# An attention block gated by a gated feed-forward block on one core: x blocks, first weights and value runs placed anew

## The chip, the cores and the metric

The kernel runs on one core of one Trainium2 chip. The metric is the device time of one execution in microseconds (us). A core has TensorE (PE, matrix products, results in PSUM), VectorE (DVE), ScalarE (ACT), GpSimd (POOL) and SyncE (SP, here only the issuer of DMAs). Each engine works through its own list in order; semaphores order the engines among each other.

## The reference

Two branches share one input x of 2048 rows by 576 columns, in bfloat16. The second input B_x is not read.

```python
xn = _layernorm(x)                                  # over the 576 columns
# branch A: causal attention, 32 heads of 18, window of 256
qkv = xn @ wqkv                                     # 576 x 1728
scores = einsum(q, k) * 18 ** -0.5                  # masked: 0 <= i - j < 256
s = (softmax(scores) @ v) @ wo                      # 576 x 576
# branch B: gated feed-forward, F = 4608
h = sigmoid(xn @ w_gate) * (xn @ w_up)
g = silu(h @ w_down)
out = x + s * g
```

## The kernel before

The 2048 rows are cut into four chunks of 512 rows, each of four blocks of 128. For each chunk the program makes: the layer norm and the transposed copy `xnT` of its blocks; q, k and v; scores, exponentials and masks per group of four heads; the products of probabilities and values, called runs here (`build_pv`, L817); the output projection; the gate and up products over 36 blocks of 128 feed-forward columns (`build_ffn`); the down products; and the final combination and store.

All contractions over the 576 columns are split into one remainder of 64 and four groups of 128. A matmul uses half of the array's rows (64), and two of them run side by side as a pair (`pair`, L127), so one line of the kernel, L127, carries nearly all products. `turn` does the four main groups first (half 0) and, in a second call (half 1), the four groups again with the halves swapped, and the remainder last. The remainder's columns of x lie twice in `xnT`, once for each half of the array: that is what `ln:dup` (L561) makes by copying 64 columns of the normalized block (`xnr`).

**The order of the work** is not written by hand. Every operation is an `Op` with an engine, an estimated time, dependencies, a priority and, for PE, a PSUM buffer that it must get from a `Pool`. `schedule` plays the program through with these estimates and fixes each engine's list. A lower `prio` goes first among operations that could start at about the same time. SP's list of DMAs comes from the same planner, with an estimated issue time and an estimated landing (`slack` corrects it). There are four PSUM units: 0 and 1 for scores and the like, 2, 3 and 1 for the feed-forward part.

**The opening.** In the first chunk x comes by four DMAs (`load_x`, x0 to x3). Each block goes through statistics (L541 to L547 on DVE; x2's on ACT, `act_stats`, L600 to L604), the inverse root on POOL (L549), the normalization (L557), the copy of 64 columns (L561), ten transposes on PE (L613: five groups times two halves) and one copy from PSUM to `xnT` (`f_xe`, L590; ACT for x0 to x2, DVE for x3). Until then PE multiplies zeros (`warm`). The first two feed-forward blocks (`NEARLY`) are made one x block at a time (`PARTS`), each part as soon as its x block is there; the third block follows over all 512 rows, with its half 0 started ahead. Gate and up weights come in groups of two feed-forward blocks (`weights`, two loads of 256 KB), their remainders for four blocks (`load_rem`, two loads of 64 KB). SP's order at the start is x0, x1, x2, x3, gate and up of group 0, two remainders, gate and up of group 1, two remainders of the next four blocks, group 2, group 3, then the attention weights.

**The runs.** Two runs per chunk, eight in all, each of 192 matmuls and as many weight loads (128 in the first chunk's). They are short instructions, so a run uses up instructions faster than any other work. Instructions come in blocks of 256 through a DMA queue of their own (66 blocks of 16 KB in the trace). `fits` refuses a start of a run if, by the planner's estimate, too little time lies between a fixed point 256 + 64 instructions ahead of a block's edge and the edge itself (`FETCH_NS`, the second value near the end of a chunk's gate and up products).

Of the kernel before, what the change touches and what calls it, by code (L numbers as in the profile page):

```python
# [7 lines left out]
S = 2048  # L8
# [37 lines left out]
FETCH_NS = (6200.0, 4350.0)  # L46
RUN_NS = 6.3
STEP_NS = (54.0, 30.6)
# [21 lines left out]
X_PRIO = (0, 0, 0, 0)  # L70
# [22 lines left out]
FILL_NS = 100.0  # L93
SPACE_NS = (1700, 1800, 1700, 1700)
# [62 lines left out]
class Pool:  # L157
# [12 lines left out]
    def pick(self, n, now, barred=()):  # L170
        free = []
        for u in self.units:
            if u in barred:
                continue
            h = self.last[u]
            if h is None:
                free.append((0.0, self.units.index(u), u))
            elif h.rel and all(r.idx >= 0 for r in h.rel):
                free.append((max(now, max(r.end for r in h.rel) + self.late), self.units.index(u), u))
        if len(free) < n:  # L180
            return None
        free.sort()
        got = free[:n]
        return max(g[0] for g in got), sorted(g[2] for g in got)
# [11 lines left out]
class Op:  # L196
    __slots__ = ("eng", "est", "deps", "fn", "name", "prio", "start", "end", "tok", "needs_tok",
                 "nbytes", "slack", "idx", "succs", "cidx", "odeps", "acq", "lane", "filler", "space", "ni", "run", "then")

    def __init__(self, eng, est, fn, name, deps, prio, nbytes, odeps, acq):  # L200
# [33 lines left out]
        self.then = None  # L234
        for d in self.odeps:
            assert d.eng == eng
# [22 lines left out]
class Builder:  # L259
# [40 lines left out]
    def alloc_memory(self):  # L300
# [61 lines left out]
        self.pool_f = Pool("F", [2, 3, 1], last)  # L362
        self.pool_v = Pool("V", [0, 1, 2, 3], last)

    def build_graph(self):
# [16 lines left out]
        self.op_xnT = [[] for _ in range(NC)]  # L382
        self.op_v = {}
# [60 lines left out]
    def load_rem(self, dst, srcs, name, lane, prio, deps=()):  # L444
        return [self.dma(dst[ROWS[1 - t], :], src[0:RD, :], RD * src.shape[1] * 3, name, lane + (t,), deps=deps, prio=prio)
                for t, src in enumerate(srcs)]

    def build_consts(self):
# [15 lines left out]
        self.warm(NWARM[0], z, None, 107)  # L464
# [60 lines left out]
    def build_ln(self, c):  # L525
# [3 lines left out]
        for i in range(BPC):  # L529
# [41 lines left out]
            self.ln_dup = dup  # L571
            self.r_st.release(ss, ap)
# [6 lines left out]
            h = self.pool_s.hold()  # L579

            def f_tr(eng, h=h, sn=sn):
                return self.transposes(eng, h, lambda r, o: self.xnr[r, sn, o:o + P])
            tr = op("PE", KB * 29.5, f_tr, f"tr:{st}", deps=[ap, dup, self.op_ident, war], prio=0, acq=h, ni=20)
            self.r_xn.release(sn, tr)
            if i == 0:
                self.warm(NWARM[1], None, tr, 80)

            def f_xe(e, h=h, i=i):
                dst = self.xnT[:, xs, :, i * P:(i + 1) * P].rearrange("p k (t c) -> p t k c", t=2)
                return e.activation(dst, self.tr_src(h), ACTF.Copy) if e is self.nc.scalar else e.tensor_copy(dst, self.tr_src(h))  # L590
            eng = XE_ENG[i]
            xe = op(eng, dve_ns(KB * P, 1.9) if eng == "DVE" else act_ns(KB * P), f_xe, f"xe:{st}", deps=[tr], prio=0)
            h.release(xe)
            self.op_xnT[c].append(xe)

    def act_stats(self, x_in, o_x, pr):
# [4 lines left out]
        m = op("POOL", 150, lambda e: e.tensor_scalar(nm, sx, -1.0 / D, None, ALU.mult), "ln:am", deps=[a1], prio=pr)  # L601
# [740 lines left out]
```

## Time and profile before

| | |
|---|---|
| time, median of 3 runs | 556.4 us (556.1 to 556.68) |
| profiled execution | 556.48 us, span 555.2 us |
| PE busy | 549.9 us, 99% |
| DVE, ACT, POOL busy | 325.1, 271.7, 208.8 us |
| data moved | 75.87 MB, mean 137 GB/s; 230 to 263 GB/s in the first 97 us |
| first gate and up product | 7.98 us after the span's start |
| last matmul ends | 552.7 us |

The span runs from the first to the last instruction; 1.3 us of the profiled execution lie around it. Durations of matmuls contain a modelled end, so matmuls overlap in the rows, and "busy" says that work was in flight, not that the array was full. A row of a timeline gives start, duration, engine, line, operation, output and input, shapes, the count of merged instructions, and in brackets the idle time before it and what ended it.

### The profile page before, as it was taken

To read this page: it belongs to the slowest core of one execution; us is meant where nothing else is said; L and a number is where in the kernel's file an instruction comes from. 1 tells how busy PE (TensorE), PEld (TensorE's weight loads), DVE (VectorE), ACT (ScalarE), POOL (GpSimd) and SP (SyncE) were. 2 spreads that over 40 slices of the span, in tenths; PEclk is the share of its full clock that TensorE was granted. 3 is DMA by queue.
4 is the path that set the end of the run, shared out by engine and by line. 5 is a ranking of instruction groups with operands and counts; after the bars stand their busy time and mean duration, and the time that the engine had idled before them with its cause. 6 is when DMAs were issued, how large, how long until landed. Compare 5 with 4: busy or idle time off the path is not lost.

```text
span 555.2 us, 19412 instructions
## 1 busy us (share of the span) xinstructions
PE 549.9 (99%) x8342; PEld 341.2 (61%) x8342; DVE 325.1 (59%) x782; ACT 271.7 (49%) x379; POOL 208.8 (38%) x360
## 2 busy tenths in 40 slices
PE   8999999999999999999999999999999999999998
PEld 7454455777555655577855565447877655445887
DVE  5467677745966545746565557664455657653511
ACT  4246554432566543645265563764165555765021
POOL 5634353826271230554452322745063332700300
DMA  8899999542256664462126653663013464540001
GB/s 230 234 263 239 248 241 257 150 91 59 72 164 182 198 167 132 129 161 53 32 65 193 201 162 101 185 179 87 9 34 103 119 204 138 153 134 2 20 28 46
DMA packets 141213, 75.87 MB, mean 137 GB/s; under 512 B 43676, under 2 KB 139260, under 8 KB 141128
## 3 DMA queue, kind: packets, MB, share of 16 engines
q1 hardware_dynamic: 133704, 68.71, 47.3%
q0 software_dynamic: 7424, 5.92, 4.0%
q8 instruction: 66, 1.08, 0.8%
q14 instruction: 19, 0.16, 0.1%
HBM read 63.18 MB, written 2.36 MB: 118 GB/s over the span
## 4 chain that ended last, share of the span: by engine, by line
PE 98%; DMA 1%; SPq 0%; issue 0%; DVE 0%; ACT 0%
PE ps L127 95%; PE ps L817 3%; DMA wgs<-in_B_w_up_dram 1%; SPq L290 0%; ACT thf L1087 0%; PE ps L613 0%; DVE thf L1089 0%; DVE xf L1092 0%
## 5 line engine op out<-in xcount | busy, mean ns | idle before, releaser
L127 PE MATMUL ps<-xnT,wgs 64*128 64x512 bf16 (+1 forms) x2400 | 284.0, 368 | 0.6 <-DMA wgs<-in_B_w_up_dram 0.5
L767 ACT ACTIVATE expr<-ps 128x1024 bf16<-128x1024 f32 (+4 forms) x160 | 155.0, 968 | 81.0 <-PE ps L127 80.5
L127 PEld LDWEIGHTS ps<-xnT,wgs 64*128 64x128 bf16 x2400 | 114.7, 94 | 108.6 <-issue 1.1
L127 PE MATMUL ps<-wd_sb,hT 64*128 64x288 bf16 (+2 forms) x2448 | 152.7, 276 | 0.0
L290 POOL DMA_DIRECT2D qk<-qd x160 | 82.9, 524 | 161.7 <-PE ps L127 152.9
L977 DVE SCALAR_TENSOR_TENSOR hT<-tring,ps 128x512 bf16<-128x512 bf16 x144 | 98.6, 685 | 74.2 <-ACT tring L974 72.6
L974 ACT ACTIVATE tring<-ps 128x512 bf16<-128x512 f32 x144 | 86.2, 598 | 113.9 <-PE ps L127 112.3
L127 PEld LDWEIGHTS ps<-wd_sb,hT 64*128 64x128 bf16 x2448 | 113.0, 94 | 29.4
L780 DVE TENSOR_TENSOR expr<-expr,mask 128x128 bf16<-128x128 bf16 (+2 forms) x240 | 65.2, 299 | 62.0 <-ACT expr L767 59.4
L290 POOL DMA_DIRECT2D oT<-o2T x72 | 36.8, 520 | 115.3 <-DVE ot L848 52.4
L731 POOL TENSOR_SCALAR kx<-kprev,small 128x256 bf16<-128x256 bf16 x64 | 60.1, 949 | 6.0 <-PE ps L127 5.1
L127 PE MATMUL ps<-qk,kx 64*128 64x320 bf16 (+1 forms) x704 | 59.2, 254 | 0.0
L127 PE MATMUL ps<-xnT,wgr 64*128 64x512 bf16 (+1 forms) x300 | 56.0, 367 | 0.0
L127 PEld LDWEIGHTS ps<-qk,kx 64*128 64x128 bf16 x704 | 31.9, 94 | 26.6
L127 PE MATMUL ps<-xnT,wqg 64*128 64x512 bf16 (+1 forms) x320 | 37.7, 355 | 0.0
L652 DVE CAST qd<-ps 128x1024 bf16<-128x1024 f32 (+1 forms) x20 | 22.3, 1115 | 11.1 <-PE ps L127 11.1
L845 DVE STREAM_TRANSPOSE ot<-ps 128x512 f32<-128x512 f32 x32 | 20.3, 687 | 13.9 <-PE ps L817 13.8
L127 PEld LDWEIGHTS ps<-xnT,wgr 64*128 64x128 bf16 x300 | 15.0, 94 | 16.4
L731 DVE TENSOR_SCALAR kx<-qk,small 128x512 bf16<-128x512 bf16 x64 | 21.9, 370 | 5.4 <-PE ps L127 4.9
L853 DVE STREAM_TRANSPOSE o2T<-o 128x512 bf16<-128x512 bf16 x32 | 22.6, 706 | 3.0 <-DMA oT<-o2T 2.5
L127 PEld LDWEIGHTS ps<-xnT,wqg 64*128 64x128 bf16 x320 | 15.0, 94 | 11.5 <-issue 0.4
L1080 ACT ACTIVATE thf<-ps 128x576 bf16<-128x576 f32 x12 | 7.8, 650 | 27.4 <-PE ps L127 27.4
(68 smaller groups left out, 289.3 us busy)
## 6 DMA issues: line engine op xcount, KB each, us to landing
wgs<-in_B_w_gate_dram SPq DMA_DIRECT2D x72, 256.0 KB, 3.5
wgs<-in_B_w_up_dram SPq DMA_DIRECT2D x72, 256.0 KB, 4.0
wd_sb<-in_B_w_down_dram SPq DMA_DIRECT2D x9, 576.0 KB, 6.7
wqg<-in_A_wqkv_dram SPq DMA_DIRECT2D x32, 128.0 KB, 3.8
qk<-qd POOLq DMA_DIRECT2D x100, 36.0 KB, 2.7
wgr<-in_B_w_gate_dram SPq DMA_DIRECT2D x36, 64.0 KB, 3.1
wgr<-in_B_w_up_dram SPq DMA_DIRECT2D x36, 64.0 KB, 2.9
wvo<-in_A_wqkv_dram SPq DMA_DIRECT2D x4, 576.0 KB, 4.2
```

Source lines behind the costliest of these rows:

```text
L127: res = eng.matmul(outs[i], lhs(ROWS[t], i), rhs(ROWS[t], i), start=start, stop=stop, tile_position=(64 * t, 0))
L290: o = self.op(eng, DMA_ISSUE_NS[eng], lambda e: e.dma_start(dst, src), name, deps, prio, nbytes=nbytes)
L652: return eng.tensor_copy(dst, self.both(h, n))
L731: return e.tensor_scalar(self.kx[:, sx, pos:pos + n_ // SW, t, :], src.rearrange("p (s k) -> p s k", k=SW), self.half[:, t:t + 1], None, A ...
L767: return eng.activation(self.expr[:, se, :, lo * SW:NT], self.both(h, NT)[:, :, lo * SW:NT], ACTF.Exp, scale=SM_SCALE)
L780: return eng.tensor_tensor(e_, e_, m_, ALU.mult)
L817: res = eng.matmul(outs[i][p0:p0 + VH, cols], self.v_aug[ROWS[i], o:o + VH], self.expr[ROWS[i], se, t, cols], start=m == 0, stop=m == len( ...
L845: return e.transpose(self.ot1[:, p1, :], self.halves(hp, NT, un)[i])
L853: t2 = op("DVE", dve_ns(NT), lambda e, p2=p2, p3=p3: e.transpose(self.o2T[:, p3, :], self.o2[:, p2, :]), f"ot2:{c}:{pr}:{i}", deps=[on, d3 ...
L974: th = op("ACT", act_ns(NT), lambda e: e.activation(self.tring[:, st, :], bank(h, 0), ACTF.Tanh, scale=0.5), f"th:{c}:{ft}", deps=[pg, dt_ ...
L977: mu = op("DVE", dve_ns(NT), lambda e: e.scalar_tensor_tensor(self.hT[:, ft, :], self.tring[:, st, :], 1.0, bank(h, 1), ALU.add, ALU.mult) ...
L1080: th = op("ACT", act_ns(w), lambda e: e.activation(v2(t), y2(), ACTF.Tanh, scale=0.25), f"fth:{nm}", deps=[f2, dt_], prio=0)
```

## The change

1. x3's load gets a priority of 1.8 instead of 0, so it is issued behind the loads of group 0 and their remainders.
2. For x0 to x2 the transposes and the copies to `xnT` are split: the four main groups start when the normalization is done, from PSUM unit 0, and the remainder's group follows after the copy of 64 columns, from unit 1. Products of half 0 wait for the main groups alone, those of half 1 and the projections for both (`op_xnR`). Main copies: DVE, ACT, ACT; remainder copies: DVE, ACT, ACT. x3 stays whole, on DVE.
3. The loads of group 1 wait for x0's copy of 64 columns (`ln_first`).
4. Three feed-forward blocks instead of two are made in parts; the third in two parts, x0 to x2 together and x3. The products made ahead are now those of the fourth block, in unit 0. The parts' priority grows with the block.
5. Warm products: 5 of double width, 27 of single, 8 of double; the ten behind the first transposes are gone.
6. The planner's landing estimates for the first loads, some estimated durations and the spacing of the scores (`SPACE_NS`) have other values.
7. `fits` counts from 256 + 16 instructions ahead of an edge, less 48 that may be queued, and not before the last instruction in that stretch that waited for another engine was let go (`held`). There are three limits (`FETCH_NS`): for the first chunk, for the later ones, and for the stretch behind a chunk's last gate and up products; they shrink as a run waits.

```diff
-FETCH_NS = (6200.0, 4350.0)
+FETCH_LEAD = 16
+QUEUED = 48
+FETCH_NS = (7300.0, 5900.0, 3950.0)
+RELAX_NS = 250e3
...
-X_PRIO = (0, 0, 0, 0)
+X_PRIO = (0, 0, 0, 1.8)
-XE_ENG = ("ACT", "ACT", "ACT", "DVE")
-NWARM = (43, 10)
-NEARLY = 2
-FIRST_SLACK_NS = (-800.0, -1500.0)
+XE_ENG = ("DVE", "ACT", "ACT", "DVE")
+XR_ENG = ("DVE", "ACT", "ACT")
+NWARM = ((5, 2), (27, 1), (8, 2))
+NEARLY = 3
+OPEN_NS = 2000.0
+OPEN_BYTES_PER_NS = 256.0
+X_LAT_NS = (400.0, 600.0, 900.0, 800.0)
+W_LAT_NS = (650.0, 1100.0)
-PARTS = (((0, 1), (1, 2), (2, 3), (3, 4)),) * NEARLY
+PARTS = (((0, 1), (1, 2), (2, 3), (3, 4)),) * 2 + (((0, 3), (3, 4)),)
...
-FILL_NS = 100.0
-SPACE_NS = (1700, 1800, 1700, 1700)
+OPEN_PE_NS = 150.0
+FILL_NS = 80.0
+SPACE_NS = (1600, 1900, 2200, 1600)
...
+        self.pool_a = Pool("F", [0], last)
+        self.pool_m = Pool("S", [0], last)
+        self.pool_r = Pool("S", [1], last)
...
-                self.x_dma[i][0].slack = -220.0
+                self.x_dma[i][0].lat = X_LAT_NS[i]
...
-    def warm(self, n, dep, before, est):
+    def warm(self, n, wide, dep, before, est):
-            return pair(eng, self.halves(h, P), lambda r, t: zero[r, :],
-                        lambda r, t: zero[r, :], True, True)
+            return pair(eng, self.halves(h, wide * P), lambda r, t: zero[r, :],
+                        lambda r, t: zero[r, None, :].broadcast_to([SW, wide, P]) if wide > 1 else zero[r, :], True, True)
-            w = self.op("PE", est, f_warm, f"warm:{i}", deps=[dep], prio=4, acq=None if before else h, odeps=[before], ni=4)
+            w = self.op("PE", wide * est, f_warm, f"warm:{i}", deps=[dep], prio=4, acq=None if before else h, odeps=[before], ni=4)
-            before = w
+            before = self.warm_last = w
...
+            if st == 0:
+                self.ln_first = dup
...
                 self.r_xn.release(sn, fl)
                 self.op_xnT[c].append(fl)
                 continue
-            h = self.pool_s.hold()
-
-            def f_tr(eng, h=h, sn=sn):
-                return self.transposes(eng, h, lambda r, o: self.xnr[r, sn, o:o + P])
-            tr = op("PE", KB * 29.5, f_tr, f"tr:{st}", deps=[ap, dup, self.op_ident, war], prio=0, acq=h, ni=20)
+            apart = i < BPC - 1
+            steps = ((range(1, KB), [ap, war], XE_ENG[i], self.pool_m), (range(1), [dup], XR_ENG[i], self.pool_r)) if apart else (
+                (range(KB), [ap, war, dup], XE_ENG[i], self.pool_s),)
+            for w, (ks, after, eng, pool) in enumerate(steps):
+                n, h = len(ks), pool.hold()
+
+                def f_tr(eng, h=h, sn=sn, ks=ks):
+                    return self.transposes(eng, h, lambda r, o: self.xnr[r, sn, o:o + P], ks)
+                tr = op("PE", n * 29.5, f_tr, f"tr:{st}:{w}", deps=[after, self.op_ident], prio=0, acq=h, ni=4 * n)
+
+                def f_xe(e, h=h, i=i, ks=ks):
+                    dst = self.xnT[:, xs, ks[0]:ks[-1] + 1, i * P:(i + 1) * P].rearrange("p k (t c) -> p t k c", t=2)
+                    src = self.tr_src(h)[:, :, ks[0]:ks[-1] + 1, :]
+                    return e.activation(dst, src, ACTF.Copy) if e is self.nc.scalar else e.tensor_copy(dst, src)
+                xe = op(eng, dve_ns(n * P, 1.9) if eng == "DVE" else act_ns(n * P), f_xe, f"xe:{st}:{w}", deps=[tr], prio=0)
+                h.release(xe)
+                if w == 0:
+                    self.op_xnT[c].append(xe)
+                if w or not apart:
+                    self.op_xnR.append(xe)
             self.r_xn.release(sn, tr)
-            if i == 0:
-                self.warm(NWARM[1], None, tr, 80)
-
-            def f_xe(e, h=h, i=i):
-                dst = self.xnT[:, xs, :, i * P:(i + 1) * P].rearrange("p k (t c) -> p t k c", t=2)
-                return e.activation(dst, self.tr_src(h), ACTF.Copy) if e is self.nc.scalar else e.tensor_copy(dst, self.tr_src(h))
-            eng = XE_ENG[i]
-            xe = op(eng, dve_ns(KB * P, 1.9) if eng == "DVE" else act_ns(KB * P), f_xe, f"xe:{st}", deps=[tr], prio=0)
-            h.release(xe)
-            self.op_xnT[c].append(xe)
 
     def act_stats(self, x_in, o_x, pr):
         op = self.op
         junk = self.tring[:, :, :].rearrange("p t n -> p (t n)")[:, 0:D]
         sx, nm, sq, ve = (self.act_st[:, k:k + 1] for k in range(4))
         a1 = op("ACT", act_ns(D) + 150, lambda e: e.activation(junk, x_in, ACTF.Identity, accum_out=sx), "ln:as", deps=[o_x, self.op_tab], prio=pr)
-        m = op("POOL", 150, lambda e: e.tensor_scalar(nm, sx, -1.0 / D, None, ALU.mult), "ln:am", deps=[a1], prio=pr)
+        m = op("POOL", 230, lambda e: e.tensor_scalar(nm, sx, -1.0 / D, None, ALU.mult), "ln:am", deps=[a1], prio=pr)
         a2 = op("ACT", act_ns(D) + 150, lambda e: e.activation(junk, x_in, ACTF.Square, bias=nm, accum_out=sq), "ln:aq", deps=[m], prio=pr)
-        v = op("POOL", 150, lambda e: e.tensor_scalar(ve, sq, 1.0 / D, EPS, ALU.mult, ALU.add), "ln:av", deps=[a2], prio=pr)
+        v = op("POOL", 290, lambda e: e.tensor_scalar(ve, sq, 1.0 / D, EPS, ALU.mult, ALU.add), "ln:av", deps=[a2], prio=pr)
         rs = op("POOL", 560, lambda e: e.tensor_tensor(self.arstd[:, :], ve, self.neghalf[:, :], ALU.pow), "ln:ar", deps=[v, self.op_negh], prio=pr)
         return nm, rs
 
-    def transposes(self, eng, h, src):
+    def transposes(self, eng, h, src, ks):
         res = None
-        for k in range(KB):
+        for k in ks:
             for t in range(2):
                 o = h.units[0] * 2048 + t * 1024 + k * 64
                 r = ROWS[t]
...
-        pj = self.two("qk", f"{c}:{gi}", n, h, lhs, rhs, [self.op_xnT[c], o_w, dq], n)
+        pj = self.two("qk", f"{c}:{gi}", n, h, lhs, rhs, [self.op_xnT[c], [] if c else self.op_xnR, o_w, dq], n)
...
-                               [self.op_xnT[c][i], wv, war])
+                               [self.op_xnT[c][i], [] if c else self.op_xnR[i], wv, war])
...
-            ds = [self.load_nat(self.wgs[:, sw, :, i, :], w[:, fc], f"dma:w:{c}:{wg}", ("w", sw, i), pr, [dw])
+            ds = [self.load_nat(self.wgs[:, sw, :, i, :], w[:, fc], f"dma:w:{c}:{wg}", ("w", sw, i), pr, [dw, self.ln_first if c == 0 and wg == 1 else None])
...
-                for d in ds:
-                    d.slack = FIRST_SLACK_NS[0] if wg == 0 else BUSY_SLACK_NS if wg > 6 else 0.0
-                for d in rem:
-                    d.slack = FIRST_SLACK_NS[1] if wg < 2 else BUSY_SLACK_NS if wg > 6 else 0.0
+                for d in ds + rem:
+                    d.slack = BUSY_SLACK_NS if wg > 6 else 0.0
+                    if wg < 4 and d.lat is None:
+                        d.lat = W_LAT_NS[min(wg, 1)]
-                f"dma:wd{fg}", ("wd", fg), deps=[hm[fg * FG + 2 - fg // 2]], prio=6))
+                f"dma:wd{fg}", ("wd", fg), deps=[hm[min(fg * FG + 2 - fg // 2, 31)]], prio=6))
...
-            xin = self.op_xnT[c][b0:b1]
+            xin = self.op_xnT[c][b0:b1] + (self.op_xnR[b0:b1] if half and not c else [])
...
-                   prio=3 if part is None else 1, odeps=chain[half] if part is None else list(behind), acq=acq,
+                   prio=3 if part is None else 1 + ft / 2, odeps=chain[half] if part is None else list(behind), acq=acq,
...
-                        ahead = self.pool_f.hold()
+                        ahead = self.pool_a.hold()
...
             waits[key] = max(waits.get(key, -1), d.idx)
         return {key: v for key, v in waits.items() if known.get(key, -1) < v}
 
-    def fits(self, at, n, st, places, ffn):
+    def fits(self, at, n, st, places, now, rate, waited):
         def when(p):
             if p < at:
-                return next(t0 + (p - a0) * w for a0, t0, w in reversed(places) if a0 <= p)
-            return st + TURN_NS + min(p - at, n) * RUN_NS + max(p - at - n, 0) * STEP_NS[ffn]
+                return next((t0 + (p - a0) * w, kind) for a0, t0, w, kind, held in reversed(places) if a0 <= p)
+            return st + TURN_NS + min(p - at, n) * RUN_NS + max(p - at - n, 0) * rate, now
         edge = at + (FETCH_AT - at) % FETCH
         while edge - FETCH - FETCH_AHEAD < at + n:
-            if edge > at and when(edge) - when(edge - FETCH - FETCH_AHEAD) < FETCH_NS[ffn]:
+            p = edge - FETCH - FETCH_LEAD
+            t0, kind = when(p - QUEUED)
+            for a0, _, _, _, held in reversed(places):
+                if a0 < p - FETCH:
+                    break
+                if a0 <= p:
+                    t0 = max(t0, held)
+            if p >= at:
+                t0 = max(t0, st)
+            if edge > at and when(edge)[0] - t0 < FETCH_NS[kind] * (1.0 - waited / RELAX_NS):
                 return False
             edge += FETCH
         return True
...
-                    if o.run and not self.fits(at + len(self.new_waits(o, known)) // 2, o.run, st, places, int(ffn[phase] < FETCH)):
+                    if o.run and not self.fits(at + len(self.new_waits(o, known)) // 2, o.run, st, places, kind, STEP_NS[ffn[phase] < FETCH], st - ready_t[o.cidx]):
+                    held = ready_o[o.cidx]
+                            if other.name != mine.name and any((p_, c_) < (o.prio, o.cidx) and r_ <= st + SHARE_NS
+                        held = max(held, got[2])
+                        bk = (k, o, st, units, held)
+            _, o, stt, units, held = best[1]
...
-                places.append((at, stt, o.est / o.ni))
+                places.append((at, stt, o.est / o.ni, kind, stt if o.run else held))
+                kind = 2 if ffn[phase] <= 36 else min(int(phase), 1)
...
+                if o.lat is not None:
+                    moved = max(moved, stt + o.est + 700.0) + o.nbytes / OPEN_BYTES_PER_NS
+                    o.end = moved + o.lat
```

More of the change, by code (lines that the diff above doesn't have):

```diff
@@ L176, in pick @@
             if h is None:
-                free.append((0.0, self.units.index(u), u))
+                free.append((now, self.units.index(u), u, 0.0))
             elif h.rel and all(r.idx >= 0 for r in h.rel):
-                free.append((max(now, max(r.end for r in h.rel) + self.late), self.units.index(u), u))
+                free.append((max(now, max(r.end for r in h.rel) + self.late), self.units.index(u), u, max(r.end for r in h.rel) + self.late))
         if len(free) < n:
@@ L183, in pick @@
         got = free[:n]
-        return max(g[0] for g in got), sorted(g[2] for g in got)
+        return max(g[0] for g in got), sorted(g[2] for g in got), max(g[3] for g in got)
     def take(self, hold, units):
@@ L197 @@
     __slots__ = ("eng", "est", "deps", "fn", "name", "prio", "start", "end", "tok", "needs_tok",
-                 "nbytes", "slack", "idx", "succs", "cidx", "odeps", "acq", "lane", "filler", "space", "ni", "run", "then")
+                 "nbytes", "slack", "idx", "succs", "cidx", "odeps", "acq", "lane", "filler", "space", "ni", "run", "then", "lat")
     def __init__(self, eng, est, fn, name, deps, prio, nbytes, odeps, acq):
@@ L234, in __init__ @@
         self.then = None
+        self.lat = None
         for d in self.odeps:
@@ L382, in build_graph @@
         self.op_xnT = [[] for _ in range(NC)]
+        self.op_xnR = []
         self.op_v = {}
@@ L463, in build_consts @@
         self.warm_src = zero
-        self.warm(NWARM[0], z, None, 107)
+        self.warm_last = None
+        for n, wide in NWARM:
+            self.warm(n, wide, z, self.warm_last, 100)
     def load_wq(self, c, gi):
@@ L1139, in schedule @@
         last_sc = 0.0
+        moved = OPEN_NS
         at = 2
@@ L1172, in schedule @@
                         for other in (self.pool_s, self.pool_f) if not o.run else ():
-                            if other is not mine and any((p_, c_) < (o.prio, o.cidx) and r_ <= st + SHARE_NS
+                            if other.name != mine.name and any((p_, c_) < (o.prio, o.cidx) and r_ <= st + SHARE_NS
                                                          for p_, c_, r_ in claims.get(other.name, ())):
@@ L1231, in schedule @@
                 elif o.lane is not None:
-                    lat = DMA_PE_NS if s_.eng == "PE" else 90.0
+                    lat = (OPEN_PE_NS if o.lat is not None else DMA_PE_NS) if s_.eng == "PE" else 90.0
                 else:
@@ L1237, in schedule @@
                 ready_t[s_.cidx] = max(ready_t[s_.cidx], o.end + lat)
+                if o.eng != s_.eng:
+                    ready_o[s_.cidx] = max(ready_o[s_.cidx], o.end + lat)
                 if remaining[s_.cidx] == 0 and s_.idx < 0:
```

8 lines of the change are left out of this document (4 added, 4 removed).

## The prediction

> **What bounds the kernel now.** I read the page's first part, then the chain that ended last, then the opening and a few stretches of the timeline.
>
> ```profile
> PE 549.9 (99%) x8342; PEld 341.2 (61%) x8342; DVE 325.1 (59%) x782; ACT 271.7 (49%) x379; POOL 208.8 (38%) x360
> ```
>
> TensorE (PE) is busy for all but 5.3 us of the span. The change removes no matmul of the model, so it can win only PE time that does no needed work: the opening, and holes hidden inside the "busy" figure. The chain says where these are (start us, us, what):
>
> ```profile
> 3.10 0.04 issue
> 3.14 4.71 DMA wgs<-in_B_w_up_dram
> 7.84 0.14 issue
> 7.98 1.00 PE ps L127 x26
> ...
> 86.18 2.07 PE ps L127 x17
> 88.25 0.05 issue
> ...
> 336.28 1.48 PE ps L817 x100
> 337.75 0.09 issue
> 337.84 1.06 PE ps L817 x77
> ...
> 513.28 2.40 PE ps L817 x168
> ```
>
> The first useful product starts at 7.98, released by the first up weights, which landed at 7.84. From there the chain is PE to the end. Two "issue" entries cut it, one behind the first probability-times-values run (L817, 84.3) and one inside the fifth (336.2). The PE timeline shows their true size:
>
> ```profile
> 82.72 1.46 PE L127 MATMUL ps<-xnT,wgs 64*128 64x512 bf16 x12
> 87.20 2.13 PE L127 MATMUL ps<-xnT,wgs 64*128 64x512 bf16 x16
> 336.21 2.69 PE L817 MATMUL ps<-expr,v_aug 64*19 64x320 bf16 x192
> 513.21 2.47 PE L817 MATMUL ps<-expr,v_aug 64*19 64x320 bf16 x192
> ```
>
> Matmuls come in pairs on two halves of the array. Twelve took 1.46, so a 512-column pair takes 0.216 and the modelled end adds 0.16. Sixteen should then take 8 x 0.216 + 0.16 = 1.89; they took 2.13: **0.24 lost**. The run of 192 at 336.21 took 2.69 against 2.47: **0.22 lost**. No releaser is named, so I read both as a lack of instructions, not of data.
>
> The opening rows:
>
> ```profile
> 7.62 0.43 DVE L557 TENSOR_SCALAR xnr<-x,small 128x576 bf16<-128x576 bf16 x1 [0.50 <-POOL small L604]
> 7.98 0.95 PE L127 MATMUL ps<-xnT,wgs 64*128 64x128 bf16 x24 [0.48 <-DMA wgs<-in_B_w_up_dram]
> 8.80 0.33 PE L613 MATMUL ps<-ident,xnr 64*128 64x64 bf16 x10
> 9.18 0.70 ACT L590 ACTIVATE xnT<-ps 128x640 bf16<-128x640 bf16 x1 [0.93 <-PE ps L613]
> 10.27 0.31 PE L613 MATMUL ps<-ident,xnr 64*128 64x64 bf16 x10
> 10.41 0.85 PE L127 MATMUL ps<-xnT,wgs 64*128 64x128 bf16 x24
> 10.62 0.49 DVE L590 COPY xnT<-ps 128x640 bf16<-128x640 bf16 x1 [0.22 <-PE ps L613]
> ```
>
> Twenty-four 128-column matmuls take 0.85 without a hole and 0.95 at 7.98, where the second x block is still being copied (0.10 lost). The third block's copy ends at 9.88, just before PE takes it.
>
> **Part 1: x3 behind the first weights.** The four x loads issue first, 0.43 us of SP plus a gap of 0.04 each, and all SP loads share one stream of data, 260 GB/s between 2.00 and 7.84. x3 is 144 KB: 147456 B / 260 GB/s = 0.57, and 0.47 of SP time. The up weights land 0.47 to 0.57 earlier; I take 0.55, near the data figure since the stream is full: 7.29. First product 7.43. **Gain 0.55.**
>
> Are x0 and x1 ready? x0 is normalized at 4.83 to 5.26. Now eight transposes start without the 64-column copy (0.18) and VectorE evacuates them (0.49 for five column groups, so about 0.4 for four) where ScalarE was held to 6.49 by x2's statistics: ready about 6.1. x1's normalize ends at 6.90; transposes about 6.95, evacuated on ScalarE from 7.3 (0.70 for five groups, about 0.6 for four) to 7.9. PE needs it one x0 round after 7.43, that is two FFN blocks x 9 pairs x 0.056 = 1.0, at 8.43. **The 0.10 goes too.** The evacuation of the doubled columns adds three short operations (about 0.2 each) that follow the main ones and release only the last product of each group; none waits on PE's path. x2's normalize ends at 8.05; main columns are ready at 8.1 + 0.35 + 0.6, about 9.1, instead of 9.88; needed at 9.6.
>
> **Part 2: x3 itself.** It now stands where the second remainder load stood: issued about 4.4 and landed by 4.31 + 4.1 = 8.4 (4.1: median landing of that load in the first 12 us). From x0's rows, landing to transposes is 5.54 - 2.88 = 2.66; from x3's, transposes to copied is 11.11 - 10.27 = 0.84. Ready at 11.9, instead of 11.11. The cover is the third FFN block: its first part, three x blocks wide, is 9 pairs x 0.163 = 1.46. PE reaches x3 at 7.43 + 3.02 (six rounds) + 0.45 (transposes) + 1.46 = 12.36. Slack 0.46. Without the third block this would be 1.0 late.
>
> **Part 3: the held second group.** Its gate load was issued at 4.95; now it waits for x0's doubled copy (ends 5.48). SP works in order, so queued behind it are its up load, the groups 2 and 3 and the attention weights; the order may let a remainder load of the third pair (0.58) go first, which costs the same. All shift by about 0.6. Group 1 landed at 5.59 + 4.9 = 10.5 and gets 64 KB more ahead, 0.25: 10.75. The third block wants it at 7.43 + 3.02 + 0.45 = 10.9, where before it was wanted at 12.23. Slack 0.15, the tightest step. Group 2 landed at 12.4 and was first used at 16.4: the shift is nothing there. What the hold may win is that nothing of group 1 moves while the up weights finish: between 0 (the stream serves in order) and 0.4 (if part of the 0.28 MB that moved beyond the first loads by 7.84 delayed them); I take **0.10**, near the lower end, since the up weights were asked for first.
>
> Smaller edits: splitting the third block makes 9 pairs of 0.163 plus 9 of 0.056 out of 9 of 0.216, +0.03. Wider and fewer warm products lie in time in which PE waits anyway, 0; if the clock were lost again it would show as pairs of 0.105, as before 4.4. Opening: 0.55 + 0.10 + 0.10 - 0.03 = **0.72**.
>
> **Part 4: placing the runs.** The planner now delays a run until its estimate of the instruction supply is met by larger numbers (7300 and 5900 for 6200), counted from when a waiting instruction lets go. It reorders PE only; FFN products fill. Bounds: all of 0.24 + 0.22 vanishes (-0.46), or new holes of the same size appear at other of the eight runs (+0.5 for two). Six of eight runs show none now, and the rule gets stricter, so I take **0.46**. The Trainium skill (Runtime: NRT & Kernel Launch, Instruction fetch mechanics) speaks against it: it calls the cost of crossing a 256-instruction block mostly hidden. By it this part would be 0 and the sum 0.72. The trace shows two holes of 0.24 and 0.22, so the rows decide, and the rule stands among the rivals.
>
> **Sum.** 0.72 + 0.46 = 1.18. The profiled execution took 556.48 (span 555.2 and 1.3 around it), 0.1 over the median of 556.4; so 555.3 from it and 555.2 on the median.
>
> **Rivals.**
> A. Only half comes through: the second group or x3 is late (slack 0.15 and 0.46, and single landings scatter by more), or the holes move instead of vanish. Gain 0.3 to 0.9: 555.5 to 556.1. For it: the thin slack. Against it: x0 to x2 all gain more time than they need.
> B. The placing of the runs is worth nothing: the holes come from something that no estimate of supply foresees, or stay where they are. Then only 0.72 is left: 555.7. For it: six runs with the same neighbours show no hole, so the two may be chance. Against it: both lie at the same place, within 2 us of a run. The Trainium skill's page named above (same section) is the reason to give this a chance of its own.
> C. New holes also eat the opening: 556.4.
> D. Slower: later runs push the attention chain into the tail. The last run is at 513.2, the output projection at 535.4, and behind that 12.1 us of down products (540.6 to 552.7) cover a slip. Beyond 12 us each us of slip is lost. A run refused waits a block of 256 instructions, 7.9 us among down products (0.123 a pair), 13.8 among gate and up (0.216 a pair); and the score spacing of the third chunk grows by 0.5 for each of 40 scores, up to 20 us. A slip of 16 costs 4, less the opening: 559. Against it: FFN work absorbs slips in the first three chunks, and waits of up to 13 us before runs already exist (scores end about 382.5, run at 395.5), which a new order can take back.
>
> **How the numbers follow.** A measurement of this kernel can tell about 0.2% (1.1 us) from no change. Forecast 0.56, A 0.18, B 0.07, C 0.04, D 0.15. The forecast lies just beyond 0.2%; what of it falls short is about as much as what of A goes past. Faster 0.56, same 0.29 (A, B and C), slower 0.15 (D). Low end: PE starts as early as x2 allows (9.1 less 2.0 of x0 and x1 rounds and 0.3 of transposes, 6.8 instead of 8.1: 1.3) and the holes go: 1.3 + 0.46, with 0.3 for landings, 554.3. High end: C and the first half us of D's slips, 556.9. About 0.07 is left below and 0.12 above; the forecast's own range is 554.6 to 555.8.
>
> **What would show it.** The first 64x128 product on wgs at about 7.4 instead of 7.98, with the DMA of the up weights or none as releaser; twenty-four of them in 0.85; the first product of the third block near 10.9; no PE wait on group 1 or on x3's copy over 0.2; all eight runs 2.4 to 2.5 long and no "issue" beside them in the chain; the last run before 525. Wrong if PE waits again between 10.5 and 12.5, if a run of 192 takes 2.7, or if PE idles after 540.

## The result, and the profile after

| | before | after |
|---|---|---|
| median of the runs, us | 556.67 (22 runs, 556.1 to 557.8) | 557.57 (22 runs, 556.6 to 559.5) |
| ratio after to before | | 1.0016, 95% interval 1.0008 to 1.0023 |
| profiled execution (span), us | 556.48 (555.2) | 557.35 (556.0) |

The forecast was 555.2 with a range of 554.3 to 556.9. The changed kernel is slower by 0.9 us (0.16%): the interval excludes any gain, but the loss stays under the 0.2% that the prediction took as the least that can be told from no change. Its times scatter more. The page shows PE as busy as before:

```profile
PE 550.9 (99%) x8334; PEld 339.4 (61%) x8334; DVE 324.7 (58%) x784; ACT 271.2 (49%) x380; POOL 209.1 (38%) x360
...
L135 PE MATMUL ps<-xnT,wgs 64*128 64x512 bf16 (+1 forms) x2416 | 283.7, 366 | 1.6 <-issue 1.2
```

The last column of the group line is where to look: the gate and up products stood idle for 1.6 us in all, 1.2 of them behind "issue", that is, with nothing in the profile to wait for. The chain that ended last (start us, us, what) shows where:

```profile
6.91 0.62 PE ps L135 x16
...
7.69 0.61 ACT xnT L609
...
9.11 1.89 PE ps L135 x57
11.00 1.20 issue
12.20 0.69 PE ps L135 x7
...
260.38 1.52 PE ps L839 x104
261.90 0.02 issue
261.92 1.03 PE ps L839 x63
...
375.24 0.05 issue
```

The first product starts at 6.91 instead of 7.98: more than the forecast asked. Then PE waits for ScalarE's copy of x1 (7.69, 0.61), and at 11.00, where the modelled end of its last matmul lies, it stops for 1.20. The timeline of PE and of the copies shows how odd that stop is:

```profile
6.91 0.62 PE L135 MATMUL ps<-xnT,wgs 64*128 64x128 bf16 x16 [0.20 <-DVE xnT L609]
8.34 0.23 PEld L135 LDWEIGHTS ps<-xnT,wgs 64*128 64x128 bf16 x8 [0.27 <-ACT xnT L609]
10.68 0.32 PE L135 MATMUL ps<-xnT,wgs 64*128 64x384 bf16 x1
12.20 0.82 PE L135 MATMUL ps<-xnT,wgs 64*128 64x384 bf16 x7 [1.20 <-issue]
13.20 0.49 DVE L609 COPY xnT<-ps 128x640 bf16<-128x640 bf16 x1 [1.94 <-PE ps L635]
513.98 2.47 PE L839 MATMUL ps<-expr,v_aug 64*19 64x320 bf16 x192
```

Eight equal matmuls of the third block are cut after **one**: one at 10.68, seven from 12.20. Half a pair has run. A missing operand would have held the first as well. x3's transposes and copy (13.20) queue behind. Counting PE's matmuls, weight loads and separate semaphore instructions together from the first of these on, the first instruction after the cut is number 449, which is 193 + 256: an edge, the first instruction of one of the blocks of 256 that `fits` counts (`FETCH_AT` is 193). Matmuls and weight loads alone would give 439. The only DMA packet of the instruction queue in this stretch is in the transfers of 9.8 to 11.0:

```profile
q8 instruction: 1, 0.02, 5.3%
```

5.3% of 16 engines over 1.2 us is 1.0 us of one DMA engine. In the trace that packet runs from 9.89 to 10.90, and PE goes on 1.30 behind its end.

The runs are as the forecast wanted, 2.47 like the last one at 513.98, but for the one at 260.4: its two pieces and the cut in the chain make 2.57 instead of 2.40. This cut too is at an edge, instruction 7617, and PE goes on 1.48 behind the end of that block's packet. The small cut at 375.24 is 0.23 long and lies in no run.

**Balance of the two profiled executions.** I compare each start of a PE instruction with an unbroken sequence of the same instructions from the first product on. Before, 0.19 is lost by 25 us and 1.32 later. After, 2.04 and 1.14. So: start 1.07 earlier, 1.85 more lost in the opening, 0.18 less lost later, and 0.17 of needed work that now lies behind the first product (split parts, transposes). -1.07 + 1.85 - 0.18 + 0.17 = +0.77; the span grew by 0.8.

### The profile page after: what moved, and what is told of

Read it like the earlier page. It is cut to its first block, busy times and chain, and to the rows that moved or that the text cites. A ratio compares the mean times of both kernels' runs of the same rounds, so it can differ in the third digit from the quotient of the medians.

```text
span 556.0 us, 19404 instructions
## 1 busy us (share of the span) xinstructions
PE 550.9 (99%) x8334; PEld 339.4 (61%) x8334; DVE 324.7 (58%) x784; ACT 271.2 (49%) x380; POOL 209.1 (38%) x360
## 4 chain that ended last, share of the span: by engine, by line
PE 99%; issue 0%; DVE 0%; ACT 0%
PE ps L135 95%; PE ps L839 3%; PE ps L635 0%; ACT xnT L609 0%; DVE xnT L609 0%; ACT thf L1109 0%; DVE thf L1111 0%; DVE xf L1114 0%; DVE hT L471 0%; DVE small L472 0%
## 5 line engine op out<-in xcount | busy, mean ns | idle before, releaser
L135 PEld LDWEIGHTS ps<-xnT,wgs 64*128 64x128 bf16 x2416 | 113.5, 94 | 112.1 <-issue 1.7
L135 PEld LDWEIGHTS ps<-xnT,wqg 64*128 64x128 bf16 x320 | 15.1, 94 | 12.3 <-issue 0.4
L736 DVE CAST v_aug<-ps 64x288 bf16<-64x288 f32 x32 | 14.5, 453 | 9.2 <-PE ps L135 8.6
```

The lines of the kernel that those rows point to most:

```text
L135: res = eng.matmul(outs[i], lhs(ROWS[t], i), rhs(ROWS[t], i), start=start, stop=stop, tile_position=(64 * t, 0))
L736: return eng.tensor_copy(dst, src)
```

## The experiments

The theory is that instruction supply takes back the early start: PE can't pass instruction 449 before its block of instructions has come. Its rivals are that data or a wait sets the same point, or that the loss is elsewhere. A load reports its landing in 16 shares, and counts as landed with the last. Times are medians; ratios are to the kernel before, measured beside each.

**1. The changed kernel again.** No edit.

> The changed kernel once more, for the spread of its opening. Supply theory: PE stops again exactly at its instruction 449 (193 + 256) and goes on 1.2 to 1.5 us after the 16 KB instruction transfer has ended; the hole is 0.8 to 1.8 us, wherever the weights land. Data theory (the third block waits for the second weight group or for PSUM unit 1): the hole ends within 0.3 us of the landing of the second up load or of the copy of the doubled columns, whichever is later, and not at a fixed instruction. Time 557.0 to 558.2.

557.8, ratio 1.0017 [1.0008, 1.0026], as expected. The stop is there again at the same instruction, 0.76 long, because the packet ended at 10.27 instead of 10.90. And a second appeared, in the third run (the chain):

```profile
10.95 0.76 issue
...
202.62 1.47 PE ps L839 x99
204.09 1.57 issue
205.66 1.06 PE ps L839 x78
```

It is at instruction 5825, again 193 plus a multiple of 256 in the same count. The same program, in the execution shown above, had this packet at 200.32, before the run, and no stop; here it came at 203.15, after the run's start. So the place of a stop is fixed by the program, its length is not.

**2. Narrow warm products.** One number of the change: 53 warm pairs of single width instead of 40 mixed ones, so that instruction 193 lies earlier.

```diff
-NWARM = ((5, 2), (27, 1), (8, 2))
+NWARM = ((53, 1),)
```

> The changed kernel with 53 warm products of single width (212 instructions instead of 160, about the same time on PE). Supply theory: the edge moves 52 instructions ahead in the work, into the third x round near 9.6 us, and its trigger to about 5.5; 4.1 us lie between them instead of 3.7, so the hole moves from the third block's first product to the third x round and shrinks to 0.3 to 1.1 us; time 556.4 to 557.4. Data theory: nothing changes, the hole stays at the first 64x384 product, 1.2 us, time 557.6.

558.85, ratio 1.0046 [1.0029, 1.0063]: wrong. The stop at 449 went, as expected; the packet came at 6.15. But it took 1.45, until 7.60, among the transfers of the first loads. Fifteen of the sixteen shares of the second remainder load were in by 7.25, the last at 8.66, and PE waited for it (timeline):

```profile
8.75 0.40 PE L135 MATMUL ps<-xnT,wgs 64*128 64x128 bf16 x8 [0.92 <-issue]
```

"issue" here is a late share of a load; that this share went through the same DMA engine as the packet would fit, but the traces do not name the engine. Later losses also grew, to 3.85 behind 25 us.

**3. Instruction 193 earlier still.** Warm products of 64 columns first, so that the block is asked for in the warm stretch (`warm` also learns the half width).

```diff
-NWARM = ((5, 2), (27, 1), (8, 2))
+NWARM = ((48, 0.5), (14, 2))
...
```

> The changed kernel with 48 warm products of 64 columns, then 14 of 256 (248 instructions instead of 160). Supply theory: the trigger at instruction 193 is passed at about 3.6 us, the edge at 449 is reached near 9.4, 5.8 us later, so the hole at 11.0 is gone and at the next edge (705, near 14) at most 0.4 us is lost; time 555.9 to 556.6, below the kernel before. Data theory: hole stays at the first 64x384 product, 1.2 us, time 557.6.

559.65, ratio 1.0053 [1.0037, 1.0069]: wrong in the same way. The packet ran from 5.23 to 6.24, in the middle of the first up weights: fifteen shares of these by 6.20, the last at 7.90, the first product at 8.14. No stop at 449, but the next edge (instruction 705) stopped PE for 0.8 at 15.8, and one in the first chunk's work (2753) for 1.0.

**4. The kernel before with fewer warm products,** 13 of the first 30 of double width, to bring the stop into it.

```diff
-NWARM = (43, 10)
+NWARM = (30, 10)
+NWIDE = 13
...
```

> The kernel before with its first 43 warm products made as 13 of double and 17 of single width (30 instead of 43, the same PE time, 52 instructions fewer), and ten behind the first transposes as they are. Supply theory: the trigger moves from the warm stretch at 5.5 us to the second block's transposes or the first product (7.2 to 8.0), the edge from 10.4 to about 11.3, so PE stops at instruction 449 for 0.8 to 1.8 us; time 557.4 to 558.4. Data theory: no third block in parts here, so no hole and 556.6 as before.

556.59, ratio 1.0001 [0.9992, 1.0009]: wrong. Instruction 193 moved from 5.66 to 7.38, only 3.33 before the edge, and no stop came: the packet started 0.93 behind instruction 193, where in the profile of after it took 2.91. Supply is not a fixed delay.

**5. The change with the old rule for the runs** (`fits`, limits and spacing of before; the second limit at 4.1 us, since at 4.35 the last run finds no place).

```diff
-FETCH_NS = (7300.0, 5900.0, 3950.0)
+FETCH_NS = (6200.0, 4100.0)
-    def fits(self, at, n, st, places, now, rate, waited):
+    def fits(self, at, n, st, places, ffn):
...
```

> The changed kernel with the old rule for placing runs (old limits 6.2 and 4.35, the second lowered to 4.1 because with 4.35 the last run finds no place; old score spacing). Theory O (the loss is made in the opening): the stop at instruction 449 stays, 0.6 to 1.6 us; after 25 us PE loses 1.1 to 1.5 us as in the kernel before; time 556.9 to 557.6. Rival R (the loss is made by the new placing): opening as in the changed kernel, yet the time falls to 556.4 or below.

559.21, ratio 1.0045 [1.0033, 1.0057]: slower than both kernels, as neither side expected. The opening has the stop of the change (0.77), and the seventh run stops long at instruction 13505, its packet having come at 445.75, after the run's start (chain):

```profile
444.87 1.47 PE ps L839 x98
446.34 1.81 issue
448.15 1.06 PE ps L839 x78
```

With the new opening the new rule is worth 1.6 us against this version of the old one, by the medians.

**6. The kernel before with the new rule alone** (`fits` and its limits, spacing; opening untouched).

```diff
-FETCH_NS = (6200.0, 4350.0)
+FETCH_NS = (7300.0, 5900.0, 3950.0)
-SPACE_NS = (1700, 1800, 1700, 1700)
+SPACE_NS = (1600, 1900, 2200, 1600)
...
```

> The kernel before with nothing but the new rule for placing runs and the new score spacing. Theory O: no stop in the opening, first product at 7.5 to 8.0; PE loses 1.1 to 1.6 us after 25 us, or more in single executions; time 556.2 to 557.0. Rival R: runs stop at block edges in most executions, 557.3 to 558.

558.84, ratio 1.0037 [1.0024, 1.005]: outside the ranges of both sides. With the old opening the new rule costs 2.3 us. PE's last matmul is at 552.8, hardly later than the 552.5 of before, but the span is 557.6. The last run went from 513.2 to 520.8, the output projection from 535.4 to 543.0, and with it the stores that free the buffers for reloading x (timeline, SP's queue and VectorE):

```profile
548.23 3.34 SPq L293 DMA_DIRECT2D xf<-in_A_x_dram  x2
553.69 0.53 DVE L1095 TENSOR_TENSOR xf<-xf,thf 128x416 bf16<-128x416 bf16 x2
555.01 1.31 SPq L293 DMA_DIRECT2D out_dram<-xf  x3
```

Before, the reload stood at 540.7; from the last matmul to the end of the span it took 2.7, here 4.8. This is the prediction's rival D, at a slip of 7.6.

**7. x3 first again,** the change otherwise whole.

```diff
-X_PRIO = (0, 0, 0, 1.8)
+X_PRIO = (0, 0, 0, 0)
```

> The changed kernel with x3 loaded before the first weights again. By the prediction's term the first product comes 0.55 us later than in the changed kernel, at 7.4 to 7.5, or 0.4 to 0.6 at least; theory O adds that the stop at instruction 449 depends on when the block's transfer gets its turn and is 0.5 to 1.6; time 557.0 to 558.0. If x3's place did not matter the first product stays at 6.9.

557.36, ratio 1.0016 [1.0005, 1.0027]. The first product moves back from 6.91 to 7.41, with the first up weights landing at 7.32 instead of 6.67, so x3's place is worth **0.50** at the first product. The median does not move: PE reaches the edge at 10.84 and goes on at 11.59, where the packet (end 10.21) lets it. The stop, 0.75 here, lies among x3's transposes (timeline):

```profile
11.60 0.29 PE L635 MATMUL ps<-ident,xnr 64*128 64x64 bf16 x8 [0.57 <-issue]
```

**8. Second weight group not held.**

```diff
-... pr, [dw, self.ln_first if c == 0 and wg == 1 else None])
+... pr, [dw])
```

> The changed kernel without the wait of the second weight group for x0's copy. By the prediction's term (0.10) the first product moves by less than 0.2 from 6.9, group 1 lands 0.3 to 0.6 earlier; theory O: the stop at instruction 449 stays since no weights are waited for there; time 557.2 to 558.0. If the hold is what protects the opening, the first product comes 0.3 us or more later.

557.34, ratio 1.0012 [1.0003, 1.002]. The group lands at 9.62 instead of 10.43, the first product comes at 7.07, within the scatter of landings. The packet ended at 9.85 and the stop was 0.25, not visible as a cut in the rows. By the medians the hold is worth nothing that can be measured. The profiled execution is the fastest of its twelve, 556.19: with a gap of 0.25 instead of 1.52 at the edge it is 1.2 below the profiled execution of after.

**9. The second feed-forward block in three parts,** which puts the edge one step later in the work.

```diff
-PARTS = (((0, 1), (1, 2), (2, 3), (3, 4)),) * 2 + (((0, 3), (3, 4)),)
+PARTS = (((0, 1), (1, 2), (2, 3), (3, 4)), ((0, 1), (1, 3), (3, 4)), ((0, 3), (3, 4)))
```

> The changed kernel with the second FFN block taken in three parts instead of four: its columns of x1 and x2 go in one part of 256 columns. That is 36 PE instructions fewer before the third block, so instruction 449, at which PE stopped in the profiles of the changed kernel, falls about 1 us later in the work; the price is a wait for x2 of about 0.3, since less work is there with x0 and x1 alone. Theory S (the stop is a late block of instructions, which lets PE go on at a point between 11.1 and 12.2 by the profiles so far, whatever PE does before): PE starts at 6.9, passes instruction 449 near 11.8 to 12.0 with a stop of 0 to 0.3, and the loss by 25 us falls from 1.6 to 2.0 to between 0.7 and 1.1; time 556.3 to 557.2. Rival L (data for the third block, not instructions, sets the point): PE waits again at the first product of the third block until 11.6 to 12.2, wherever instruction 449 lies, and the loss by 25 us stays at 1.6 to 2.0; time 557.4 to 557.9.

The opening did as the supply theory says, the time did not: 559.01, ratio 1.0052 [1.0034, 1.0071]. PE reached instruction 449 at 12.00 and went on at 12.38, 1.31 behind a packet that ended at 11.07. Data were not it: all eight matmuls of the third block's first part at 11.25 went through, and the cut moved with the edge:

```profile
11.25 0.81 PE L135 MATMUL ps<-xnT,wgs 64*128 64x384 bf16 x8
12.38 1.27 PE L135 MATMUL ps<-xnT,wgs 64*128 64x128 bf16 x24 [0.31 <-issue]
```

Lost by 25 us: 1.29. Behind it 2.93 went, of it 0.36 in the third and 0.56 in the last run at edges, with packets that ended 1.46 and 1.43 before PE went on.

**10. The same without the hold.**

> As the kernel with three parts for the second block, and the second weight group is not held either. Theory S: as there, stop 0 to 0.2; the group lands 0.8 earlier, which nobody waits for; time equal to that of the other within 0.3, 556.2 to 557.2. Rival L (data sets the point): the earlier group takes 0.5 to 0.8 of the wait away, so this one is faster than the kernel with the hold by about that.

557.57, ratio 1.0016 [1.0007, 1.0024]. Here the opening is clean of stops; the chain runs from 11.29 to 94.02 without a break:

```profile
11.29 82.73 PE ps L135 x882
```

The first product is at 6.85 and 0.93 is lost by 25 us (the waits for x1 and x2): together 0.4 better than before, less the 0.15 or so of needed work that now lies behind the first product. The rest of the kernel loses 1.96, 0.64 more than before, above all 0.5 at an edge in the last run. The expected difference from experiment 9 was under 0.3 and is 1.4; since this edit shifts the planner's whole order (the first run moves from 98.0 to 96.2), the runs fall elsewhere against the edges, and the two can't be compared for the hold.

**11. Two feed-forward blocks in parts** instead of three.

```diff
-NEARLY = 3
+NEARLY = 2
...
-PARTS = (((0, 1), (1, 2), (2, 3), (3, 4)),) * 2 + (((0, 3), (3, 4)),)
+PARTS = (((0, 1), (1, 2), (2, 3), (3, 4)),) * 2
```

> The changed kernel with two FFN blocks in parts instead of three, so the fourth x block is wanted directly behind the third. The prediction held that x3 would then be 1.0 late. Theory S: PE reaches x3's transposes at about 10.7 and finds x3 not ready until 11.2 to 11.7 (its landing at 7.8, 3.5 to 4 us behind it); the wait for x3 and the wait for instruction 449 lie at the same place, so they cover each other: one loss of 0.8 to 1.4 instead of the stop, loss by 25 us 1.4 to 2.0, time 557.1 to 557.9, as the changed kernel. Rival: the two waits add up, since the block of instructions is asked for later: loss by 25 us 2.4 to 3.0, time 558 to 558.8.

558.79, ratio 1.0053 [1.0034, 1.0071], 2.66 lost by 25 us: the rival, by which the two waits add. The edge falls behind the first of x3's ten transposes (timeline):

```profile
10.61 0.19 PE L635 MATMUL ps<-ident,xnr 64*128 64x64 bf16 x1
12.07 0.30 PE L635 MATMUL ps<-ident,xnr 64*128 64x64 bf16 x9 [1.27 <-issue]
12.96 0.86 PE L135 MATMUL ps<-xnT,wgs 64*128 64x128 bf16 x24 [0.59 <-DVE xnT L609]
```

x3's transposes stand behind the stop, so its copy, and the wait of 0.59 for it, come on top. The third block covers those 0.59.

**12. Part 1 alone:** the kernel before, x3 behind the first weights.

```diff
-X_PRIO = (0, 0, 0, 0)
+X_PRIO = (0, 0, 0, 1.8)
```

> The kernel before with one thing of the change: the fourth x block is loaded behind the first weights. Theory (the 0.55 of the prediction is right for the start, and the third block is what lets it be kept): first product at 7.4 to 7.5 instead of 7.98; PE reaches x3's transposes at about 9.8 and waits 1.0 to 2.0 for them; loss by 25 us 1.2 to 2.2 instead of 0.2; time 556.7 to 557.8. Rival (the x loads are ready anyway, and the early start is kept): the wait at x3 is under 0.3, time 555.8 to 556.3.

The start is as expected, 7.49, and 1.65 is lost by 25 us; the time, 561.51 (ratio 1.0087 [1.0073, 1.0101]), is not. Yet the start is no earlier than the 7.48 and 7.61 of experiments 4 and 6, which load x3 first. The up weights land at 6.89 instead of 7.31 and 7.34, but this kernel's PE takes x1's transposes (7.31) ahead of the first product. Both waits of experiment 11 are in the opening again:

```profile
10.88 0.51 PE L127 MATMUL ps<-xnT,wgs 64*128 64x128 bf16 x11 [0.51 <-issue]
...
12.45 0.86 PE L127 MATMUL ps<-xnT,wgs 64*128 64x128 bf16 x24 [0.59 <-DVE xnT L590]
```

Then the new order of the rest loses 5.35: among others 1.4 in the sixth run at an edge (381.29) and 0.9 at 533.5, where PE waits for ScalarE. One number in the opening changed the planner's order of the whole kernel.

**What the runs give together.** In the fourteen profiles, 27 gaps of over 0.23 us between two starts of PE lie exactly at an edge. In three of them the packet had ended 4.1 to 11.2 us before, and PE was held by other work. In the other 24 PE goes on **1.23 to 1.58 us after the end of that block's packet**. The opening's edge, at instruction 449:

| kernel | instruction 193 | packet | PE could go on (end + 1.4) | PE there | stop |
|---|---|---|---|---|---|
| before | 5.66 | 7.69 to 8.66 | 10.1 | 10.42 | none |
| after | 6.98 | 9.89 to 10.90 | 12.3 | 10.68 | until 12.20 |
| after again | 6.93 | 9.22 to 10.27 | 11.7 | 10.62 | until 11.70 |
| x3 first | 7.00 | 9.25 to 10.21 | 11.6 | 10.84 | until 11.59 |
| no hold | 7.15 | 8.68 to 9.85 | 11.2 | 10.84 | until 11.08 |
| three parts | 7.04 | 10.03 to 11.07 | 12.5 | 12.00 | until 12.38 |
| three parts, no hold | 6.92 | 8.83 to 9.79 | 11.2 | 11.88 | none |
| two blocks | 6.92 | 9.62 to 10.64 | 12.0 | 10.61 | until 12.07 |
| before, x3 late | 5.88 | 8.46 to 9.46 | 10.9 | 10.15 | until 10.87 |

The packet starts 1.5 to 3.0 us behind instruction 193 in these rows, 1.7 in experiment 3, and 0.3 to 0.9 in experiments 2 and 4. Over all edges of the fourteen traces its start lies between 2.0 ahead of the instruction one block before the edge and 4.1 behind it, with a median of 0.2. What sets this I could not settle: it is long in the stretch where the weight loads fill the DMA engines, but experiment 4 asks in that stretch too and gets its block in 0.93.

## Why the prediction was wrong, by its own steps

- **x3 behind the first weights, 0.55: right in size, 0.50** (experiment 7). Landings agree: the first up weights land at 7.31 to 7.34 in experiments 4, 6 and 7, with x3 first, and at 6.26 to 6.89 in nine profiles with x3 behind them (in experiment 3, where the packet fell among them, at 7.90). Without the split copies it starts nothing earlier (experiment 12). The first product came a further half earlier, at 6.91 and not 7.43, because the base of 7.98 was a late one: in the profile of before the last share of the up weights landed at 7.84, the fifteenth at 6.96. One packet of 512 bytes took 1.0 in this stretch, which may be the reason. Two kernels with the same order of loads start at 7.48 and 7.61 (experiments 4 and 6). One execution's start was taken for the kernel's.
- **The 0.10 hole at x1: not won.** PE now asks for x1 at 8.07, and its copy ends at 8.30; 0.27 is lost instead.
- **x3 under the cover of the third block: right in kind.** Nothing waits for x3's copy in after. Without the third block 0.59 is lost, not 1.0.
- **The hold, +0.10: nothing** (experiment 8). The slack of 0.15 was read well: the group landed at 10.43, PE took it at 10.68.
- **Opening sum, 0.72: the step that failed.** It added an earlier start, shorter instructions and fewer warm products and asked of data alone whether PE would be fed. In before, PE took 4.76 from instruction 193 to 449, with idle time and warm products among them; in after it takes 3.69, and starts 1.3 later. The packet, with its 1.4 behind it, does not fit in. So the opening, with the start, the losses and the added work of the balance, cost 0.95 where 0.72 was to be won. The prediction used this very mechanism for the runs in Part 4 and did not put the question to the opening, whose instructions are short as well. Its own sign for being wrong, PE waiting again between 10.5 and 12.5, is what happened, but not for group 1 or x3, the two causes that it had named.
- **Runs, 0.46: mis-sized and half misread.** The 0.22 in the run at 336.2 was at an edge (9921; packet ended at 336.49, PE went on at 337.85). The 0.24 at 87.85 was not: it lies between half 0 and half 1 of one product, is 0.23 in every profile that has it, and is at 375.24 in after. The matmul rows name no releaser, but the row of the weight loads in before, which the prediction did not show, names PE itself:

```profile
88.29 0.55 PEld L127 LDWEIGHTS ps<-xnT,wgs 64*128 64x128 bf16 x8 [0.56 <-PE ps L127]
```

I read it as a wait of half 1 on the half directly before it; no rule for runs touches it. What came is 0.18 in the one execution, and 1.6 lost again in the next. What the rule is worth depends on the order it meets: 1.6 won against the old rule in the new opening (experiment 5), 2.3 lost in the old one (experiment 6).
- **Rivals.** A to C were nearest: C has the opening eaten, at 556.4, but gives it no stop longer than the gain, and the measured 557.57 lies beyond it. D is real but did not strike here: the last run only slipped to 514.0. Its cover is smaller than the 12.1 worked out from the down products: at a slip of 7.6 the tail is already 2.1 longer, since the reload of x waits for stores (experiment 6).
- **The Trainium skill** (Runtime: NRT & Kernel Launch, Instruction fetch mechanics) calls the crossing of a block's edge mostly hidden. Most edges in these traces do pass unseen, about 24 in 900 stopping PE by the count above, so the word "mostly" agrees; where short instructions follow each other the runs show 0.2 to 2.0 us for one crossing, and there the measurement decides.

The median is not explained by the stop alone. Experiment 10 is free of it and still measures 557.57, its gain in the opening being lost in the last run and at waits of one half on the other. That profile, at 556.96, is the fastest execution of its kernel, and those of experiments 7 and 8 are 0.7 and 1.2 below their medians; where the median executions lose the rest is not shown. Shown is that the early start is taken back at instruction 449 in after, and that each order has losses of its own at edges further on. No version tried beats the kernel before.

## What to carry to other kernels

Before crediting an earlier start, count the instructions behind it: where an engine runs through a block of 256 in less time than the supply of the next one needs, the start only moves the wait. The time alone is no rule: experiment 4 runs through its block in 3.33 without a stop, because its packet came soon. Take the base of a sum from more than one execution if a single late packet can set it, and look whether a small hole returns at the same pair of instructions before calling it chance or supply. In a kernel ordered by a planner, one number in the opening reshuffles everything behind it, so a gain of half a microsecond has to be larger than what the reshuffle costs.

## What the hardware showed

- A block of instructions is one packet of 16 KB that takes 0.9 to 1.8 us in the fourteen traces. In the two profiles in which the first such packet fell among the first weights, one share of a load came late: 15 of 16 shares by 7.25 and the last at 8.66 in experiment 2, by 6.20 and at 7.90 in experiment 3. There, asking earlier for instructions cost data; that packet and share met on one DMA engine is inferred.
- At the 24 stops PE goes on 1.23 to 1.58 us after the end of the packet, not at it.
- Three of the long stops in runs (1.4 to 2.0 us) came where the packet started after the run did (203.15, 380.05 and 445.75, for runs that began at 202.54, 379.8 and 444.8). In the profile of after, the first of these packets came at 200.32, for the same program, without a stop. That the request hangs behind PE's last wait before the run would fit, but nothing here tests it.
